# A list scheduler that counts TensorE's instructions in blocks of 256

## The chip, the cores and the metric

The kernel runs on one core of one Trainium2 chip. The metric is the time of one execution on the device in microseconds (us), as the median of several runs. Beside it stands one execution that the hardware profiler took, whose span runs from the first to the last instruction of the program.

## The reference

Four layers run one after the other on a sequence of 2048 rows with 512 columns, each as x = x + layer(layernorm(x)). Layer A multiplies a two-dimensional spectrum by a learned filter; layer B is a long convolution, whose kernel K is made from a state-space model and is the same in both B layers.

```python
def _A_ref(x, w_r, w_i):
    X = rfft2(x) * (w_r + 1j * w_i)
    return irfft2(X, s=(S, D))

def _B_ref(u, A_re, A_im, B_re, B_im, C_re, C_im, log_dt, Dskip):
    dt = exp(log_dt)[:, None]
    P = exp((dt * A)[:, :, None] * arange(L))
    K = einsum("dn,dnl,dn->dl", C, P, dt * B).real
    Kf, Uf = rfft of K and of u, both padded to 2L
    return irfft(Uf * Kf)[:L] + u * Dskip

x = x + _A_ref(_layernorm(x), ...)
x = x + _B_ref(_layernorm(x), ...)
x = x + _A_ref(_layernorm(x), ...)
x = x + _B_ref(_layernorm(x), ...)
```

Here A, B and C in the einsum are complex. All inputs and the output are float32.

## The kernel before

Every Fourier transform is written as matmuls with small tables of cosines and sines, in two factors with a product by twiddles between. The whole of x stays on chip; spectra and intermediate tiles go through DRAM and come back in another layout.

The work is cut into pieces, each a Python generator that yields what its next step needs: an engine's name, a buffer ring, a bank of PSUM, or an event. The class Clock keeps a rough time for each engine (`free`), for each buffer and for the transfers (`land`, with eight transfers open at once). `run` looks for the pieces whose next step could start soonest, takes the one of lowest rank among those within 0.1 us of the earliest, emits its instructions, and lets `note` move the engines' times on. Nothing of this runs on the chip: it only settles in which order each engine's instructions stand, and the chip then follows that order engine by engine, waiting on semaphores. So a number in Clock changes the program only by the order that comes of it.

One thing depends on these times beside the order. Where `run` sees that TensorE would stand idle for over a microsecond before its next step, `fill` puts in matmuls of a 128x128 table on itself (L398), whose result nobody reads. There are 245 of them in the program.

The pieces that the prediction speaks of belong to layer B, which runs twice (r = 0 and r = 1, with r = 1 near the end of the program). The 512 columns go in two halves, e = 0 and e = 1.

- `forward_b`, eight steps b per half: matmuls of the normed x (L813), two copies by ScalarE (L815), and a transfer to DRAM (L831), issued by ScalarE for odd b, otherwise by SyncE (SP).
- `group_b`, eight groups q per half: the spectrum, 16 matmuls (L846); two products with the convolution's spectrum by VectorE (L945); their sum and difference by GpSimd (L951); 32 matmuls back (L962), into all four PSUM banks of their kind; four copies by ScalarE (L971).
- In the layer r = 0 with e = 1 each group also makes its part of the convolution's spectrum: SP loads it from the tile yk into one of three buffers (L924), TensorE runs 16 further matmuls of L846 (on wk), and ScalarE copies the result and stores it (L931, L932). In the layer r = 1 it is loaded (L921).
- `turn_k` makes the last quarter of yk (L1284, stores L1307): none of the loads at L924 may start before all eight stores of it have landed.
- `inv_b`, eight steps b per half: once all eight groups of a half are copied, a load of 512 KB (L981) into one of four buffers, by ScalarE for odd b and by SP otherwise; 8 matmuls (L993); VectorE adds to x (L999); in the layer r = 1 ScalarE issues the store of the result (L1016).

On SP and on ScalarE a transfer that waits for its buffer holds up all that stands behind it. A float32 matmul is carried out in two passes, each with its own load of weights: the trace shows 64 passes for 32 matmuls.

Of the kernel before, what the change touches and what calls it, by code (L numbers as in the profile page):

```python
# [8 lines left out]
BF = mybir.dt.bfloat16  # L9
# [31 lines left out]

RANK = -4, 0.3, 6, 1.2, 25, 0.5, 24, 0.5

NEAR = 0.1

FILL = 1.0, 0.6, 0.25
# [151 lines left out]
class Clock:  # L198
# [4 lines left out]
    def __init__(self, net, last=None):  # L203
        self.net, self.n = net, len(net.nc.cur_bb.bb.instructions)
        self.free, self.seen, self.events, self.marks, self.drops = {}, {}, {}, [], []
        self.held, self.slots, self.land, self.piece, self.table, self.form = {}, {}, 0.0, None, "", None
        self.pools = []
        self.lanes = last.lanes if last else [0.0] * 8
        if last:
            self.free, self.seen, self.events, self.land, self.table = last.free, last.seen, last.events, last.land, last.table  # L210

            self.held = {k: h for k, h in last.held.items() if h[0] in ("ge", "gl", "kh")}
            self.slots.update((k, last.slots[k]) for k in ("ge", "gl", "kh"))
# [68 lines left out]
    def take(self, engine, start, us):  # L282
        self.free[engine] = start + us

    def note(self, ready):

        listed = self.net.nc.cur_bb.bb.instructions
        end = ready
        for ins in listed[self.n:]:
            if not ins.outs or not hasattr(ins.outs[0], "bass_ap"):  # L290
                continue
            engine = {"Activation": "ACT", "Pool": "POOL"}.get(ins.engine.name, ins.engine.name)
            if engine not in COST:
                continue
            aps = [(a.bass_ap, w) for l, w in ((ins.ins, False), (ins.outs, True)) for a in l if hasattr(a, "bass_ap")]
            boxes = [(a.tensor.name, self.boxes(a), w) for a, w in aps]
            start = self.free.get(engine, 0.0)
            for name, box, w in boxes:
                for other, t, v, by in self.seen.get(name, ()):
                    if (w or v) and t > start and (w != v or box[0][2] > 1) and engine != by and self.meet(box, other):  # L300
                        start = t
            out = ins.outs[0].bass_ap
            n = max(int(np.prod([b for _, b in a.ap[1:]])) for a, _ in aps)
            fixed, each, hop = COST[engine]
            if ins.opcode.startswith("DMA"):
                both = all(str(a.space) != str(DRAM) for a, _ in aps)
                start = max(start, self.lanes[0])
                self.land = max(self.land, start) + out.nbytes() / RATE[both]
                done = self.land + LAND
                self.lanes = self.lanes[1:] + [done]  # L310
                self.take(engine, start, COST["SP"][0])
            else:
                if engine == "PE":
                    n = int(np.prod([b for _, b in out.ap[1:]]))
                    stat, rows = aps[1][0], out.ap[0][1]
                    if aps[0][0].dtype == BF:
                        each *= 0.25
                    elif rows < 128:
                        fixed, each = fixed + (0.015 if rows > 32 else -0.005), each * max(rows, 32) * stat.ap[0][1] / 128 ** 2
                    elif stat.ap[0][1] < 128:  # L320
                        fixed, each = fixed + 0.03, each * stat.ap[0][1] / 128
                    elif stat.ap[-1][0] > 2:
                        each *= 2
                    form = rows, stat.ap[0][1]
                    fixed, self.form = fixed + 0.1 * (form != self.form), form
                elif engine == "ACT":
                    each *= 1.75 if out.ap[-1][0] > 8 else 1.55 if len(aps) > 3 else 1
                    f = str(ins.func).split(".")[-1] if ins.opcode == "Activation" else "Copy"
                    if f not in (self.table, "Copy", "Identity", "Abs", "Square"):
                        fixed, self.table = fixed + 1.28, f  # L330
                elif engine == "DVE":
                    wide = sum(int(np.prod([b for _, b in a.ap[1:]])) > 1 for a, _ in aps)
                    memory = not any(str(a.space) == str(PSUM) for a, _ in aps)
                    if ins.opcode == "Reciprocal":
                        each = 6.3
                    elif ins.opcode == "TensorScalarPtr" and wide < 3 and memory:
                        fixed, each = fixed + 0.13 * (len(aps) > wide), 0.53
                    if memory and ins.opcode[:2] != "BN":
                        for a, b in self.pools:
                            start = b if a <= start < b else start  # L340
                if engine == "POOL":
                    self.pools = self.pools[-15:] + [(start, start + fixed + each * n / 1000)]
                self.take(engine, start, fixed + each * n / 1000)
                done = self.free[engine] + hop
            for name, box, w in boxes:
                self.seen.setdefault(name, []).append((box, done, w, w and engine == "PE" and engine))
                if len(self.seen[name]) > 48:
                    self.seen[name] = [e for e in self.seen[name] if e[1] > ready - 3]
            end = max(end, done)
        self.n = len(listed)  # L350
        for key in self.marks:
            self.events.setdefault(key, []).append(end)
        self.marks = []
        return end
# [46 lines left out]
    def run(self, plan):  # L401

        pieces = [[rank, i, 0.0, (), piece] for i, (rank, piece) in enumerate(plan)]
        while pieces:
            ready = [(t, p) for p in pieces if (t := self.time(p[2], p[3])) is not None]
            assert ready, [p[4].__name__ for p in pieces]
            now = min(t for t, _ in ready) + NEAR
            t, p = min((e for e in ready if e[0] <= now), key=lambda e: e[1][:2])
# [1117 lines left out]
```

## Time and profile before

| | us |
|---|---|
| three runs | 768.06, 772.99, 772.9 |
| median of the runs | 772.9 |
| the profiled execution, its own time | 770.48 |
| span of the profiled execution | 768.7 |

The mean clock that TensorE was granted in the span is 0.978 of full speed. In a row of the timeline stand the start, the time that it took, the engine, the line, the operation, the tiles, the shape and the number of passes; in brackets follows the idle time of the engine just before and what ended it. "issue" there is time for which the profile shows nothing that the engine waited for. PE is TensorE, PEld its loads of weights, DVE VectorE, ACT ScalarE, POOL GpSimd. A q after an engine's name is its sequencer, which issues transfers.

### The profile page before, as it was taken

The page shows a single profiled execution, that of the slowest core. Times are in us where ns is not written, and L with a number is a line of the kernel's source. Part 1 is how long each engine was busy: PE and PEld are TensorE (multiplying, and loading weights), DVE is VectorE, ACT ScalarE, POOL GpSimd, SP SyncE. Part 2 cuts the span into 40 slices and gives each one's busy share as a digit, 9 for nine tenths or more (in the row PEclk, how much of TensorE's full clock was granted, in tenths as well). Part 3 has the DMA queues.
Part 4 walks back from the last instruction along what each step waited for, and adds up shares of the span by engine and source line. Part 5 has one row for each costly group of instructions (what it writes and reads, how often), then busy time and mean ns, then how long its engine had stood idle before and what let it go on. Part 6 is the DMA issues. An engine that isn't in the chain of part 4 may idle for free. (4 is left out here: it accounts for less than half of the span.)

```text
span 768.7 us, 24184 instructions
## 1 busy us (share of the span) xinstructions
PE 675.8 (88%) x10382; PEld 460.0 (60%) x10382; DVE 494.8 (64%) x896; ACT 416.1 (54%) x759; POOL 305.0 (40%) x339
## 2 busy tenths in 40 slices
PE   7989998898998899897998789888898999897986
PEld 6877766656565444555455446777777645553666
DVE  6596877957966858863453534876676688275613
ACT  5776998798897797644333032275543434232120
POOL 3921454616625333300343322274544652086310
PEclk9999999999999999999999899999999999999899
DMA  9705312451442977359897953920667235966749
GB/s 331 243 22 177 118 43 104 138 171 69 137 141 95 323 226 237 113 166 239 200 268 226 267 150 89 302 113 4 240 240 245 80 85 122 210 201 182 197 103 285
DMA packets 76699, 132.56 MB, mean 172 GB/s; under 512 B 4684, under 2 KB 53584, under 8 KB 75952
## 3 DMA queue, kind: packets, MB, share of 16 engines
q1 hardware_dynamic: 59184, 103.74, 43.5%
q10 hardware_dynamic: 17408, 27.27, 13.4%
q8 instruction: 82, 1.34, 0.7%
q14 instruction: 25, 0.20, 0.1%
HBM read 70.31 MB, written 27.13 MB: 127 GB/s over the span
## 5 line engine op out<-in xcount | busy, mean ns | idle before, releaser
L1203 POOL TENSOR_TENSOR Y<-wk,Y 128x1024 f32<-128x1024 f32 x32 | 64.5, 2016 | 91.8 <-issue 37.6
L951 POOL TENSOR_TENSOR wk<-wk 128x512 f32<-128x512 f32 x32 | 40.0, 1271 | 113.4 <-DVE wk L945 111.3
L398 PE MATMUL ps<-cRa 128*128 128x128 f32 x490 | 68.7, 288 | 6.4 <-DMA cRa<-in_cRa_dram 4.6
L398 PEld LDWEIGHTS ps<-cRa 128*128 128x128 f32 x490 | 60.8, 196 | 21.0 <-issue 13.9
L945 DVE TENSOR_TENSOR wk<-ps,Y 128x1024 f32<-128x1024 f32 x32 | 37.5, 1218 | 55.5 <-PE ps L846 33.8
L993 PE MATMUL ps<-wk,cRbT 64*128 64x256 f32 x512 | 61.6, 387 | 7.1 <-DMA wk<-Ya 6.2
L815 ACT COPY wk<-ps 128x512 f32<-128x512 f32 x64 | 36.9, 589 | 52.8 <-PE ps L813 43.6
L993 PEld LDWEIGHTS ps<-wk,cRbT 64*128 64x128 f32 x512 | 52.2, 190 | 17.0 <-issue 10.9
L813 PE MATMUL ps<-wk,cRb 128*32 128x256 f32 x1024 | 59.8, 381 | 1.4 <-DVE wk L538 1.0
L1188 DVE SCALAR_TENSOR_TENSOR wk<-wk,ps 128x1024 f32<-128x1024 f32 x32 | 38.8, 1214 | 28.9 <-ACT wk L1186 28.8
L945 DVE TENSOR_TENSOR Y<-ps,wk 128x1024 f32<-128x1024 f32 x32 | 37.4, 1219 | 26.9 <-issue 23.8
L1172 ACT ACTIVATE Y<-ps 128x1024 f32<-128x1024 f32 x48 | 46.6, 1027 | 8.0 <-PE ps L1156 7.9
L813 PEld LDWEIGHTS ps<-wk,cRb 128*32 128x32 f32 x1024 | 34.9, 109 | 26.2 <-DVE wk L538 3.4
L999 DVE TENSOR_TENSOR x<-x,ps 128x256 f32<-128x256 f32 x64 | 24.8, 408 | 38.7 <-PE ps L993 38.5
L762 PE MATMUL ps<-cDaT,apart 128*32 128x256 f32 (+1 forms) x256 | 46.0, 328 | 1.4 <-DVE wk L1227 0.9
L951 POOL TENSOR_TENSOR wk<-Y 128x512 f32<-128x512 f32 x22 | 27.5, 1274 | 45.5 <-DVE Y L945 37.1
L1216 PEld LDWEIGHTS ps<-Y 128*32 128x32 f32 x2048 | 31.2, 112 | 23.7 <-issue 14.0
L1156 PE MATMUL ps<-wk,Y 96*128 96x512 bf16 x128 | 40.2, 388 | 5.5 <-DVE Y L1199 3.8
L971 ACT COPY Ya<-ps 128x256 f32<-128x256 f32 x64 | 19.3, 386 | 44.4 <-PE ps L962 29.3
L1216 PE MATMUL ps<-Y 128*32 128x64 f32 x2048 | 36.3, 223 | 7.7 <-POOL Y L1204 2.8
L1191 ACT ACTIVATE wk<-wk,quarter 128x1024 f32<-128x1024 f32 x32 | 36.8, 1148 | 8.7 <-DVE wk L1189 8.6
L962 PE MATMUL ps<-wk,Y 32*32 32x256 f32 x1344 | 34.8, 399 | 7.6 <-issue 3.9
(218 smaller groups left out, 1668.7 us busy)
## 6 DMA issues: line engine op xcount, KB each, us to landing
Y<-in_GA_dram SPq DMA_DIRECT2D x12, 899.0 KB, 9.3
x<-in_PA_dram SPq DMA_DIRECT2D x16, 642.0 KB, 3.9
x<-in_A_x_dram SPq DMA_DIRECT2D x16, 512.0 KB, 9.5
wk<-yk SPq DMA_DIRECT2D x16, 512.0 KB, 12.5
wk<-khat SPq DMA_DIRECT2D x16, 512.0 KB, 6.5
yk<-wk SPq DMA_DIRECT2D x24, 256.0 KB, 2.9
kd<-wk SPq DMA_DIRECT2D x4, 1024.0 KB, 3.9
khat<-wk SPq DMA_DIRECT2D x8, 512.0 KB, 4.4
```

The source lines that it names most:

```text
L398: self.net.nc.tensor.matmul(p[:, :128], R, R, start=True, stop=True)
L762: nc.tensor.matmul(p[32 * i:32 * i + 32, o:o + n], self.folded(r, i)[:, b, s2].rearrange("p g m -> p (g m)"), self.DaT[:, b, first:first + ...
L813: self.nc.tensor.matmul(p[o:o + 32, 256 * h:256 * h + 256], self.Rb[:, 2 * h + j, 32 * a:32 * a + 32], xn[s], start=True, stop=True)
L815: self.nc.scalar.copy(y[:, j, :], p)
L945: nc.vector.tensor_tensor(t[c], x, kh[:, :, ::-1, :] if c else kh, op=OP.mult)
L951: nc.gpsimd.tensor_tensor(Z[:, :, c], t[0][:, :, c], t[1][:, :, c], op=op)
L993: nc.tensor.matmul(q[s], self.RbT[o, i, :], y[o, i, :], start=i == 0, stop=i == 3)
L1156: self.nc.tensor.matmul(p, f[:, c:c + 128], self.oh[:k, o:o + 512], start=True, stop=True)
L1172: nc.scalar.activation(m[:, :, 1024:] if i == 2 else m[:, i, :1024], p.rearrange("p (i m) -> p i m", i=2) if i == 2 else p, AF.Exp)
L1188: nc.vector.scalar_tensor_tensor(s, c, MAGIC, p, op0=OP.subtract, op1=OP.subtract)
L1203: nc.gpsimd.tensor_tensor(E[:, 0, :1024], c, m[:, :1024], op=OP.mult)
L1216: nc.tensor.matmul(pk[32 * j:32 * j + 32, 64 * e:64 * e + 64], E1[:, r, i, :], E2[:, r, i], start=r == 0, stop=r == 1)
```

## The change

`note` now calls a new method `words` for each step of TensorE. It adds the step's instructions, two for a bfloat16 matmul and four for any other, to a count. When the count passes 256, the step may start no sooner than a time that was noted at the block before; and a new such time is noted for the next block: 2 us behind the later of this start and `land`, the time at which the last transfer that has been issued so far will be in. No instruction, wait or transfer is added or taken away by hand. `last.fetch` carries the count over from the first half of the program to the second.

```diff
+FETCH = 256
 NEAR = 0.1
...
         self.pools = []
+        self.fetch = last.fetch if last else [0, 0.0, 0.0]
...
+    def words(self, start, n):
+
+        self.fetch[0] += n
+        if self.fetch[0] >= FETCH:
+            self.fetch[0] -= FETCH
+            start = max(start, self.fetch[2])
+            self.fetch[1:] = start, max(start, self.land) + 2.0
+        return start
...
+                if engine == "PE":
+                    start = self.words(start, 2 if aps[0][0].dtype == BF else 4)
                 if engine == "POOL":
```

Up to the tail of the convolution's kernel the order stays as it was, and so it does from the second layer A to the start of the last layer B. GpSimd's order is the same throughout. What moves lies in three places: two groups of matmuls near the end of the kernel's making change places, and both layers B are ordered anew. Of the matmuls at L398 199 stand there in place of 245, and 45 of the 46 that are missing belong to the first layer B, the last to the second. In the changed file each line stands 13 lower: L398 is L411, L846 is L859, L962 is L975, L981 is L994, L993 is L1006.

In the first layer B, on TensorE, the piece around the first five inverse steps, before (8 matmuls of L993 are one step):

```order
L846 MATMUL ps<-Ya,Y 32x256 x16
L846 MATMUL ps<-wk 32x256 x16
L993 MATMUL ps<-wk,cRbT 128x256 x8
L846 MATMUL ps<-Ya,Y 32x256 x16
L993 MATMUL ps<-wk,cRbT 128x256 x8
L398 MATMUL ps<-cRa 128x128 x3
L993 MATMUL ps<-wk,cRbT 128x256 x16
L846 MATMUL ps<-wk 32x256 x16
L962 MATMUL ps<-wk,Y 32x256 x32
L846 MATMUL ps<-Ya,Y 32x256 x16
L962 MATMUL ps<-wk,Y 32x256 x32
L993 MATMUL ps<-wk,cRbT 128x256 x8
```

and the same piece now:

```order
L859 MATMUL ps<-wk 32x256 x32
L859 MATMUL ps<-Ya,Y 32x256 x16
L975 MATMUL ps<-wk,Y 32x256 x32
L859 MATMUL ps<-Ya,Y 32x256 x16
L1006 MATMUL ps<-wk,cRbT 128x256 x40
L859 MATMUL ps<-wk 32x256 x32
L975 MATMUL ps<-wk,Y 32x256 x32
L859 MATMUL ps<-Ya,Y 32x256 x16
```

The five inverse steps stand in one row of 40 matmuls, the groups before and behind them are drawn together, and the three matmuls of L398 are gone.

On SP, the loads of yk (L924) and those of the inverse steps (L981) at the same place, before:

```order
L924 DMA wk<-yk 128x2x512
L981 DMA wk<-Y 128x1x1024 x3
L924 DMA wk<-yk 128x2x512 x2
L981 DMA wk<-Y 128x1x1024
L924 DMA wk<-yk 128x2x512 x2
```

and now:

```order
L937 DMA wk<-yk 128x2x512 x2
L994 DMA wk<-Y 128x1x1024 x2
L937 DMA wk<-yk 128x2x512 x2
L994 DMA wk<-Y 128x1x1024 x2
L937 DMA wk<-yk 128x2x512
```

One load of yk moves ahead of the first loads of the inverse steps, one of the inverse loads moves behind two loads of yk, and another load of yk moves ahead of the last pair.

In the second layer B, on TensorE, where the groups of the half e = 1 meet the inverse steps of e = 0, before:

```order
L846 MATMUL ps<-Ya,wk 32x256 x16
L993 MATMUL ps<-wk,cRbT 128x256 x16
L846 MATMUL ps<-Ya,wk 32x256 x16
L993 MATMUL ps<-wk,cRbT 128x256 x16
L846 MATMUL ps<-Ya,wk 32x256 x16
L962 MATMUL ps<-wk,Y 32x256 x32
L846 MATMUL ps<-Ya,wk 32x256 x16
L962 MATMUL ps<-apart,Y 32x256 x32
L993 MATMUL ps<-wk,cRbT 128x256 x8
```

and now:

```order
L975 MATMUL ps<-wk,Y 32x256 x32
L1006 MATMUL ps<-wk,cRbT 128x256 x8
L859 MATMUL ps<-Ya,wk 32x256 x16
L1006 MATMUL ps<-wk,cRbT 128x256 x32
L859 MATMUL ps<-Ya,wk 32x256 x16
L975 MATMUL ps<-wk,Y 32x256 x32
L859 MATMUL ps<-Ya,wk 32x256 x16
L975 MATMUL ps<-apart,Y 32x256 x32
```

The last of the five inverse steps of the half moves up to the other four, ahead of the groups that it followed.

## The prediction

> **What bounds the kernel now.** I read the page first, for how full each engine is and what the instruction queue moves.
>
> ```profile
> PE 675.8 (88%) x10382; PEld 460.0 (60%) x10382; DVE 494.8 (64%) x896; ACT 416.1 (54%) x759; POOL 305.0 (40%) x339
> ...
> q8 instruction: 82, 1.34, 0.7%
> ```
>
> TensorE is busy for 88% of the span. Its matmuls and loads of weights are 2 x 10382 = 20764 instructions, and the queue of instructions moved 82 packets: 253 instructions to a packet, so blocks of 256 with some waits in them fit. Then the windows of the two places that the change orders anew, the first layer B and the end of the second.
>
> ```profile
> 404.00:428.00 24.00, 15.77 (x466) 9.53 (x456) 7.07 (x6) 7.84 (x19) 8.98 (x8) 0.93 0.86 237
> 428.00:455.00 27.00, 24.58 (x469) 14.94 (x464) 14.85 (x26) 5.54 (x12) 7.50 (x6) 0.88 0.82 229
> 455.00:476.00 21.00, 18.19 (x476) 11.43 (x474) 7.07 (x6) 7.69 (x22) 7.49 (x6) 0.99 0.23 74
> 701.00:741.00 40.00, 34.36 (x788) 21.91 (x782) 17.98 (x23) 9.65 (x33) 18.05 (x15) 0.91 0.64 161
> ```
>
> After the length come busy times of TensorE, its loads, VectorE, ScalarE and GpSimd, then the granted clock, the share of the DMA engines and GB/s. Until 455 the transfers fill 0.82 to 0.86 of the DMA engines, then 0.23, while TensorE is never idle for long: up to 455 two things could bound this stage, behind it TensorE's order alone. The timeline of TensorE shows where it stands still.
>
> ```profile
> 418.53 0.88 PE L846 MATMUL ps<-Ya,Y 64*32 64x256 f32 x23 [1.40 <-issue]
> 419.04 0.38 PE L846 MATMUL ps<-wk 64*32 64x256 f32 x1
> 419.18 0.45 PE L846 MATMUL ps<-Ya,Y 64*32 64x256 f32 x7
> 419.26 1.23 PE L846 MATMUL ps<-wk 64*32 64x256 f32 x31
> 420.42 1.50 PE L962 MATMUL ps<-wk,Y 32*32 32x256 f32 x64
> 421.84 0.62 PE L846 MATMUL ps<-Ya,Y 64*32 64x256 f32 x2
> 427.84 1.53 PE L846 MATMUL ps<-Ya,Y 64*32 64x256 f32 x23 [5.38 <-issue]
> ...
> 429.18 2.33 PE L846 MATMUL ps<-wk 64*32 64x256 f32 x31
> ...
> 451.45 1.31 PE L846 MATMUL ps<-wk 64*32 64x256 f32 x24 [2.33 <-issue]
> ```
>
> Both of the first holes lie inside a row of like matmuls, with nothing that they wait for, and between them stand 23+1+7+31+64+2 = 128 passes, with their loads 256 instructions: one block. So these are waits for instructions, 9.1 us in this stage. The queue of SP shows what each stood behind.
>
> ```profile
> 404.05 0.36 SPq L924 DMA_DIRECT2D wk<-yk  x1
> ...
> 416.93 3.35 SPq L981 DMA_DIRECT2D wk<-Y  x3
> 420.39 5.19 SPq L924 DMA_DIRECT2D wk<-yk  x2
> 439.33 0.54 SPq L981 DMA_DIRECT2D wk<-Y  x1
> 439.92 2.65 SPq L924 DMA_DIRECT2D wk<-yk  x2
> ```
>
> The block that begins at 418.53 asks for the next one just when the inverse steps' loads of 512 KB have been issued; it comes 9.3 us later. The hole at 451.45 follows loads at 439.33 and 439.92 likewise. For the second place there is the chain of work that ended last (it begins at 533.93 only).
>
> ```profile
> 704.74 1.74 PE ps L962 x49
> 706.48 3.66 issue
> 710.14 1.09 PE ps L962 x10
> ...
> 725.93 0.99 ACTq L1016
> ...
> 727.48 2.03 PE ps L962 x57
> ...
> 741.77 11.33 DMA wk<-Ya
> ```
>
> Again a hole of 3.66 us, then a wait of 1.63 for ScalarE's copies, which stood behind stores of the result in ScalarE's queue, and at the end the loads of the last half. What ends earlier before 741 ends the kernel earlier.
>
> [...]
>
> **The change part by part.** No instruction is added; all comes from the order.
>
> *The two groups at the end of the kernel's making.* The same steps change places within some 10 us. I take 0, ends -1 and +1.
>
> *The first layer B up to 404.* TensorE has the same work before the last L1284, and the first load of yk waits for the last store of that row (404.05). 45 of the 46 matmuls of L398 that go stand in this layer, with two passes each. Their cost:
>
> ```profile
> 457.68 1.83 PE L398 MATMUL ps<-cRa 128*128 128x128 f32 x14
> ...
> 404.00:428.00 24.00, 3.48 (x24) 2.90 (x24) 0.93 0.86 237
> 428.00:476.00 48.00, 7.40 (x52) 6.25 (x52) 0.93 0.56 162
> ```
>
> The first row is of the timeline, 0.13 us a pass; the others are the windows of L398 alone. Those before 404 cover a wait for transfers and are worth nothing: TensorE will be idle there in their place. A hole of 1.40 (at 418.53) may fall into that wait; I take -1 for this part, ends 0 and -2.
>
> *The hole of 5.38.* Counting four instructions to a matmul along the rows, the start of a block that stood at 427.84 now falls at the end of the spectrum of group 2, and the block before it begins just behind the last group of the first half, whose copies release the loads L981. So the large hole comes again, at about the same time: 0, ends -3 and +4.
>
> *From there to the end of the stage.* It lasts from 427.84 to the first step L993 of the next stage, with these rows in it:
>
> ```profile
> 437.27 3.72 PE L993 MATMUL ps<-wk,cRbT 64*128 64x256 f32 x32
> 440.92 1.09 PE L846 MATMUL ps<-wk 64*32 64x256 f32 x32
> ...
> 452.69 2.38 PE L962 MATMUL ps<-wk,Y 32*32 32x256 f32 x64
> ...
> 456.25 1.50 PE L962 MATMUL ps<-wk,Y 32*32 32x256 f32 x64
> ...
> 460.39 0.73 PE L962 MATMUL ps<-wk,Y 32*32 32x256 f32 x32 [0.89 <-POOL wk L951]
> ...
> 474.34 0.73 PE L962 MATMUL ps<-wk,Y 32*32 32x256 f32 x32 [0.50 <-POOL wk L951]
> 475.00 1.35 PE L993 MATMUL ps<-wk,cRbT 64*128 64x256 f32 x10
> ```
>
> Before: 11 sets of L846 at 1.09, 7 of L962 at 1.50 and 5 inverse steps at 1.86 are 31.8 us. The stage takes 475.00 - 427.84 = 47.2. The other 15.4 are L398 (7.4), the hole of 2.33, six waits for GpSimd and ScalarE (2.8, the first and last shown) and slow passes behind holes (2.9; 2.38 against 1.50). Now one spectrum of L846 more is done ahead of the hole, and part of another, so 9 sets remain: 9.8 + 10.5 + 9.3 = 29.6, with 18 passes of L398 (2.6). The hole, the waits and the slow passes I keep: 2.3 + 2.8 + 2.9. That makes 40.2, a gain of 7.0. Ends: -2, if all of L398 was cover and waits take its place; -15, if hole, waits and slow passes go too.
>
> Behind TensorE here stand ScalarE's copies, and behind these the loads of the next stage, so it moves with this end.
>
> *The second layer B.* The fifth inverse step moves ahead of the groups. The block now begins about as the loads L981 are issued, not after, so its hole of 3.66 should go; but the first inverse step then waits for its own load, which landed some 7.5 us after its issue, of which groups cover about 5. The copies behind ScalarE's stores come later than the stores, so most of the 1.63 goes as well: -3.66 - 1.63 + 2.5, about -3. Ends: +3 (a larger hole in the next block) and -6 (all of it goes and the wait is covered).
>
> The sum: 0 - 1 + 0 - 7 - 3 = -11. From the profiled execution's own 770.5 (span 768.7) that gives 759.5. The median of the runs, 772.9, is 2.4 above the profiled one and the lowest run 2.4 below it, so I forecast 760.
>
> **The rivals.** *Transfers set the end.* All eight loads of yk, eight stores of the spectrum and eight loads of the inverse steps, 12.6 MB, pass between 404 and 455 at 229 to 237 GB/s, 53 us if nothing else moves; the new order moves the same bytes. For it speaks 0.82 to 0.86; against it, that TensorE needs 21 us more behind 455, at 0.23. Then L398's place is taken by waits, the first layer gives 2 and the second nothing: 768 to 769.
>
> *The fifth step's load holds TensorE.* The inverse steps have four buffers, so the fifth load starts when the first step is done, in the first layer on SP behind two loads of yk; and TensorE stands with groups ready behind it. The DMA issues give the times to landing:
>
> ```profile
> wk<-yk SPq DMA_DIRECT2D x16, 512.0 KB, 12.5
> ...
> wk<-Y SPq DMA_DIRECT2D x8, 512.0 KB, 11.9
> ...
> 667.33 3.53 PE L846 MATMUL ps<-Y 64*32 64x256 f32 x64 [2.06 <-DMA Ya<-wk]
> ```
>
> Three steps cover 5.6 us. With 11.9 to landing, and 5.2 more for the issue at 420.39 in the first layer, the waits are 11.5 and 6.3. Each idle time of 2 us or more brings slow passes (3.53 against twice 1.09): 1.4 each. That is 20.6 less the 11 of the forecast: 780. It decides from a landing of about 10 us on, where it takes the whole gain. Against it: by then the first four loads are in, and a load into a quieter queue lands sooner.
>
> [...]
>
> [...] A hole of 5.38 us is followed by 31 passes in 2.33 us against 1.23 before it. [...]
>
> **How the numbers follow.** The forecast has 0.58, the transfers 0.24, the waits that are not there 0.06, the fifth load 0.12. The own range of the forecast is 750 to 766: its lower end with the hole of 2.33, the waits and 2 us of the second layer gone too, its upper with +4 at the large hole and half of the second layer's gain. The range for 8 in 10 is 750 to 776; it holds the two cases without change and stops short of 780. One per cent, about what a measurement of this kernel can tell from no change, is 7.7 us around 772.9: faster is below 765.2. That is the forecast's 0.58; the same are the 0.24 and 0.06, so 0.30; slower 0.12.
>
> **What would show it.** Right: in the new profile the stage from the first load of yk to the first matmul of the following stage is 7 to 9 us shorter, L398 has 398 passes, one hole of 4 to 8 us remains inside a row of L846 or L962 near the loads of the inverse steps, and in the last layer no hole of over 3 us stands between those loads and the next copies. Wrong: TensorE waiting for a load at the row of five inverse steps, or waits of several us for the loads of yk where L398 stood, or holes as many and as long as before.

## The result and the profile after

| | before | after |
|---|---|---|
| median of 20 runs each, us | 771.27 | 763.22 |
| lowest to highest, us | 765.94 to 776.4 | 755.68 to 768.87 |
| span of the profiled execution, us | 768.7 | 763.5 |
| granted clock over the span | 0.978 | 0.974 |

The ratio of the runs is 0.9889, with a 95% interval of 0.9865 to 0.9913: the changed kernel is 6.7 to 10.4 us faster. Ratios here and below compare fast runs alone, without executions at a lower granted clock (one of the 20 of the changed kernel, 768.87 at 0.967), so they can differ from the ratio of the medians. All its lines stand 13 lower (L846 is L859, L962 is L975, L993 is L1006, L398 is L411, L924 is L937, L981 is L994, L1016 is L1029).

The page of the changed kernel, TensorE's busy time and the queue of instructions:

```profile
PE 669.8 (88%) x10290; PEld 452.5 (59%) x10290; DVE 496.0 (65%) x896; ACT 416.7 (55%) x759; POOL 305.1 (40%) x339
...
q8 instruction: 81, 1.33, 0.7%
```

TensorE has 92 passes fewer, all of them L398 (490 before, 398 now). To see where they went, take the first layer B as one window, from its first pass of L846 to the first pass of the long row of inverse steps that ends it; this window is called the stage below. Of before, all instructions and then L398 alone:

```profile
363.83:475.00 111.17, 95.50 (x2141) 55.54 (x2141) 49.11 (x59) 32.73 (x80) 39.95 (x32) 0.94 0.76 204
...
363.83:475.00 111.17, 17.82 (x124) 14.97 (x124) 0.94 0.76 204
```

Of the changed kernel the same window and L411 alone:

```profile
366.21:472.78 106.57, 89.33 (x2050) 49.09 (x2051) 49.51 (x59) 32.76 (x81) 39.94 (x32) 0.89 0.81 215
...
366.21:472.78 106.57, 5.63 (x34) 4.57 (x34) 0.89 0.81 215
```

The first number behind the length is TensorE's busy time. The stage is 4.6 us shorter, and the sum shows three things. L398 went from 17.82 to 5.63: 12.2 less. Idle time, the length less the busy time, went from 15.67 to 17.24: 1.6 more. And the remaining passes, the same 2016 in number, went from 95.50 - 17.82 = 77.7 to 89.33 - 5.63 = 83.7: 6.0 more, at a granted clock of 0.89 in place of 0.94. So idle time was not what the new order took away. These are two profiles; the table behind the experiments has nine.

What TensorE waited for in this window, before and after, by the view of waits (total us, times, longest):

```profile
PE ps L846 <- issue: 13.0, 4, 5.4
PE ps L962 <- POOL wk L951: 2.9, 6, 0.9
```

```profile
PE ps L859 <- issue: 9.7, 3, 5.3
PE ps L975 <- issue: 4.6, 5, 2.1
PE ps L975 <- ACT Y L984: 3.3, 1, 3.3
...
PE ps L975 <- POOL wk L964: 0.7, 2, 0.4
```

"issue" is time in which TensorE waited for nothing that the profile shows; inside a row of like matmuls it is a hole. The sums are 13.0 before and 9.7 + 4.6 after, but 3.86 and 3.47 of them stand just ahead of the first pass of the window; inside it the holes are 9.1 before and 10.8 after. The change plans for these waits, yet as many remain. The timeline of TensorE shows them, and what became of the places that the prediction spoke of:

```profile
393.51 2.35 PE L975 MATMUL ps<-wk,Y 32*32 32x256 f32 x46 [3.33 <-ACT Y L984]
397.94 1.11 PE L975 MATMUL ps<-wk,Y 32*32 32x256 f32 x18 [2.08 <-issue]
...
425.59 1.28 PE L975 MATMUL ps<-wk,Y 32*32 32x256 f32 x39 [0.77 <-issue]
...
429.07 1.07 PE L859 MATMUL ps<-Ya,Y 64*32 64x256 f32 x25 [0.31 <-ACT Y L944]
435.45 1.07 PE L859 MATMUL ps<-Ya,Y 64*32 64x256 f32 x7 [5.31 <-issue]
...
440.54 9.27 PE L1006 MATMUL ps<-wk,cRbT 64*128 64x256 f32 x80
...
456.59 0.71 PE L975 MATMUL ps<-wk,Y 32*32 32x256 f32 x27 [0.73 <-issue]
...
472.78 1.57 PE L1006 MATMUL ps<-wk,cRbT 64*128 64x256 f32 x12
```

The large hole is there again, 5.31 us, inside a row of L859 (25 passes, hole, 7 passes). The five inverse steps at 440.54 run in one row with no wait. From the end of the large hole to the end of the stage it takes 472.78 - 435.45 = 37.3 us, against 47.2 before. The queue of SP says what stood in flight:

```profile
407.58 0.36 SPq L937 DMA_DIRECT2D wk<-yk  x1
...
424.07 1.25 SPq L994 DMA_DIRECT2D wk<-Y  x2
428.00 2.45 SPq L937 DMA_DIRECT2D wk<-yk  x2
442.60 4.31 SPq L994 DMA_DIRECT2D wk<-Y  x2
```

From the first load of yk to the end of the stage it is 472.78 - 407.58 = 65.2 us, before 475.00 - 404.05 = 70.95.

In the second layer B nothing was gained: from its first spectrum to the last row of group matmuls it takes 735.28 - 662.10 = 73.2 us, before 739.71 - 667.33 = 72.4. The timeline of TensorE and that of ScalarE in the changed kernel, where before the hole of 3.66 and the wait of 1.63 stood:

```profile
707.94 0.70 PE L1006 MATMUL ps<-wk,cRbT 64*128 64x256 f32 x3
711.26 6.85 PE L1006 MATMUL ps<-wk,cRbT 64*128 64x256 f32 x61 [2.62 <-issue]
...
723.49 2.91 PE L975 MATMUL ps<-apart,Y 32*32 32x256 f32 x64 [1.91 <-ACT Ya L984]
```

```profile
719.16 3.77 ACTq L1029 DMA_DIRECT2D out_dram<-x  x2
722.97 1.20 ACT L984 COPY Ya<-ps 128x256 f32<-128x256 f32 x4 [17.47 <-DMA wk<-Y]
```

A hole of 2.62 now stands inside the second of the five inverse steps, and the copies at 722.97 still stand behind two stores of the result.

### The profile page after: what moved, and what is told of

It is laid out like the page before. It is cut to its first block, busy times and chain, and to the rows that moved or that the text cites. A ratio compares the mean times of both kernels' runs of the same rounds, so it can differ in the third digit from the quotient of the medians.

```text
span 763.5 us, 24003 instructions
## 1 busy us (share of the span) xinstructions
PE 669.8 (88%) x10290; PEld 452.5 (59%) x10290; DVE 496.0 (65%) x896; ACT 416.7 (55%) x759; POOL 305.1 (40%) x339
## 5 line engine op out<-in xcount | busy, mean ns | idle before, releaser
L964 POOL TENSOR_TENSOR wk<-wk 128x512 f32<-128x512 f32 x32 | 39.9, 1273 | 107.6 <-DVE wk L958 98.4
L1006 PE MATMUL ps<-wk,cRbT 64*128 64x256 f32 x512 | 60.6, 382 | 8.2 <-DMA wk<-Ya 5.0
L1006 PEld LDWEIGHTS ps<-wk,cRbT 64*128 64x128 f32 x512 | 52.3, 187 | 16.6 <-issue 9.1
L411 PE MATMUL ps<-cRa 128*128 128x128 f32 x398 | 57.3, 294 | 4.7 <-DMA cRa<-in_cRa_dram 4.7
L411 PEld LDWEIGHTS ps<-cRa 128*128 128x128 f32 x398 | 51.4, 203 | 15.4 <-issue 9.2
L975 PE MATMUL ps<-wk,Y 32*32 32x256 f32 x1344 | 38.1, 409 | 9.8 <-issue 5.4
L964 POOL TENSOR_TENSOR wk<-Y 128x512 f32<-128x512 f32 x22 | 27.5, 1273 | 45.1 <-DVE Y L958 33.7
L1169 PE MATMUL ps<-wk,Y 96*128 96x512 bf16 x128 | 40.3, 388 | 5.6 <-DVE Y L1212 3.8
L984 ACT COPY Y<-ps 128x256 f32<-128x256 f32 x64 | 19.3, 389 | 41.5 <-PE ps L975 34.9
```

The source lines that it names most:

```text
L411: self.net.nc.tensor.matmul(p[:, :128], R, R, start=True, stop=True)
L964: nc.gpsimd.tensor_tensor(Z[:, :, c], t[0][:, :, c], t[1][:, :, c], op=op)
L975: nc.tensor.matmul(v[j][h][i:i + 32], gi[o:o + 32, j, 4 + 2 * s + c, :], Z[o:o + 32, j, c, :], start=c == 0, stop=c == 1)
L1006: nc.tensor.matmul(q[s], self.RbT[o, i, :], y[o, i, :], start=i == 0, stop=i == 3)
L1169: self.nc.tensor.matmul(p, f[:, c:c + 128], self.oh[:k, o:o + 512], start=True, stop=True)
```

## The experiments

To mix the two orders, the kernels below take the steps from a written list in place of the planner's choice. The list has two parts, one for each call of `run`, and names for each step its piece, its buffers and the matmuls of L398 ahead of it. With the list of before it gives the instructions of the kernel before, with that of after those of the changed kernel.

```diff
     def run(self, plan):
-            now = min(t for t, _ in ready) + NEAR
-            t, p = min((e for e in ready if e[0] <= now), key=lambda e: e[1][:2])
...
+        for step in ORDER[self.turn].split():
+            i, slot, fill = step.split(":")
+            p = pieces[int(i)]
```

At several points both kernels have done the same steps, in another order, so that a stretch of one list can stand in the other. In these kernels L839, L955, L986, L917 and L393 are the L846, L962, L993, L924 and L398 of before (two lines lower in the two kernels that are moved by half a block); likewise L944, L964 and L974 are L951, L971 and L981, and L924 where it names a copy by ScalarE is L931.

**The changed order in the first layer B alone.**

```diff
-ORDER = before[0], before[1]
+ORDER = before[0], before[1][:180] + after[1][180:356] + before[1][356:]
```

> The changed order in the first layer B alone (from the first loads of yk and the turns that go before them to the first step of the following stage, 176 steps of the list, with 17 matmuls of L398 instead of 62); everywhere else the order of before. Theory A (the gain comes from this stage, and what the two traces gave back elsewhere is no gain): 8 us less than before, ratio 0.988 to 0.992, as much as the whole change. Theory B (the prediction's sum: first layer 8, second layer 3): the same here, 8 less, and then some 3 us more in the changed kernel than here. Theory C (the gain is spread over many small moves): 3 to 5 less. In the profile, by A and B: the stage ends 7 to 10 us earlier, a hole of 4 to 6 us remains inside a row near the loads of the inverse steps.

Measured: 0.992 of before (0.9884 to 0.9956), a median of 761.3 us. The window of the stage:

```profile
365.61:469.37 103.76, 89.66 (x2050) 49.84 (x2050) 49.99 (x59) 32.55 (x80) 40.09 (x32) 0.90 0.82 221
```

It is 7.4 us shorter than that of before. So most of the gain comes from this stage, as theories A and B have it. The runs alone don't exclude theory C: of its 3 to 5 us, 3.4 to 5 lie inside the interval (3.4 to 8.9 us). And not all that this profile gains is in the stage: the second layer B, whose order is untouched, takes 69.5 us in it for 72.4 before (a table below has this length for other kernels).

**The changed order at the end of the kernel's making alone.**

```diff
-ORDER = before[0], before[1]
+ORDER = after[0], before[1]
```

> The changed order at the end of the kernel's making alone (two stretches of the list, 25 and 12 steps); everywhere else the order of before, with 444 matmuls of L398. Theory A: 0 to +2 us, since the profile of the changed kernel lost 1.8 us between 257 and 301 with a new idle time of 0.90 us. The prediction's term: 0, ends -1 and +1. Rival: a part of the gain comes from here, -2 to -4, if what TensorE does later in the first layer B is set by the copies and stores that this stage issues.

Measured: 1.0023 (0.9983 to 1.0062), of 771.3 us so 1.3 us less to 4.8 more. No gain comes from here. (The expectation gives a count of 444 for L398; it stands at 490 passes, as before.)

**The changed order in the second layer B alone.**

```diff
-ORDER = before[0], before[1]
+ORDER = before[0], before[1][:867] + after[1][867:]
```

> The changed order in the second layer B alone (the last 144 steps of the list); everywhere else the order of before. The prediction's term: -3 us (ends +3 and -6). Theory A, from the two traces (72.7 us before, 73.5 after in this layer): -1 to +1, the hole of 3.66 us goes and a hole of 2.6 us and a wait of 1.9 us come in its place. Rival: the block boundaries lie elsewhere here than in the changed kernel, since the 46 matmuls of L398 that stand ahead are not gone, so the same order has other holes and gives up to 3 either way.

Measured: 1.005 (1.0011 to 1.0089), slower by 0.8 to 6.9 us. The timeline of TensorE, at the place where the changed kernel has 2.62:

```profile
708.26 0.72 PE L955 MATMUL ps<-wk,Y 32*32 32x256 f32 x27
714.25 2.14 PE L955 MATMUL ps<-wk,Y 32*32 32x256 f32 x37 [5.26 <-issue]
```

The same order has another hole at another matmul, and a longer one: 45 matmuls of L398 that the changed kernel leaves out in the first layer are still ahead of it. This is the rival of the expectation, with a loss.

**The order of before without L398 in the first layer B.** The 62 matmuls of L398 there are left out; nobody reads their result.

```diff
-ORDER = before[0], before[1]
+ORDER = before[0], before[1][:180] + [no_fill(s) for s in before[1][180:356]] + before[1][356:]
```

> The order of before, with the 62 matmuls of L398 in the first layer B left out (they write a bank that nobody reads) and no other step moved. Theory A (the gain comes from the order and the holes; the matmuls of L398 mostly covered waits): -1 to -3 us of the 8. Rival (the matmuls of L398 stood on the path, and the new order gains by having fewer of them): -6 to -8, as much as the change. Third: without them TensorE is idle for longer and runs slower behind the waits, 0 to +3.

Measured: 1.0001 (0.9967 to 1.0036). The window of the stage, and the first two rows of its waits:

```profile
365.38:472.47 107.09, 82.92 (x2016) 43.10 (x2017) 49.40 (x59) 32.83 (x80) 39.95 (x32) 0.90 0.80 216
```

```profile
PE ps L955 <- POOL wk L944: 7.0, 8, 2.6
PE ps L986 <- issue: 4.5, 1, 4.5
```

Without L398 the idle time is 107.09 - 82.92 = 24.2 us, against 15.7, and the waits for GpSimd are 7.0 in place of 2.9; the same 2016 passes take 82.9 in place of 77.7. Of the 17.8 us that L398 took, 13.7 came back as waits and slower passes in this profile, and the runs show no gain over the whole kernel: they exclude the 8 us. In the changed kernel the waits for GpSimd are 0.7 (3.7 in the profile of its order in this stage alone), with 34 passes of L398 left: other work stands in its place. But the stage itself is not as long as before in this profile. Its 107.09 us lies 4.1 under the 111.17 of before, while the second layer B, where nothing was changed, takes 3.1 more (75.5 for 72.4). So the runs say that the absence of L398 doesn't gain the 8 us over the whole kernel; they don't say that the stage gains nothing by it.

**Half a block further, the changed kernel and the kernel before.** The list stays; of the 24 matmuls of L398 at the start 8 become 40 small ones, so that every later instruction stands 128 further on.

```diff
-        for _ in range(n):
+        for _ in range(n if start else n - 8):
             self.net.nc.tensor.matmul(p[:, :128], R, R, start=True, stop=True)
+        for _ in range(0 if start else 8 + 32):
+            self.net.nc.tensor.matmul(p[:32, :64], R[:, :32], R[:, :64], start=True, stop=True)
```

> The changed kernel, every step in its order, with its instructions moved by half a block: of the 24 matmuls of L398 at the start 8 are replaced by 40 small ones (32 x 64), 32 matmuls or 128 instructions more, in a place where TensorE waits for the first input. Theory A (the holes inside rows are waits for the next 256 instructions): they stand 64 passes earlier in the list than in the changed kernel, so the one of 5.31 us is no longer at the same matmul; the time is that of the changed kernel within 4 us, since the gain comes from real work where L398 stood. Theory B (the gain needs the block boundaries where the list put them): 4 to 8 us more than the changed kernel, near 770. Theory C (holes are not bound to blocks): the hole stays at the same matmul.

> The kernel before, every step in its order, moved by half a block in the same way. Theory A: holes 64 passes earlier in the list; the hole of 5.38 us gets smaller or goes, since its block is asked for before the four loads of the inverse steps are issued, and others come; the time within 4 us of before. Theory B: anything from -6 to +6, as the boundaries happen to fall; a gain of 6 or more would say that the change gained by where the boundaries fell. Theory C: the hole stays at the same matmul and the time is that of before within 1 us.

Measured: 0.9962 (0.992 to 1.0004) for the changed order and 1.0065 (1.0029 to 1.0101) for that of before. Both start later; the first pass of `turn_k` in before and in this version of before:

```profile
150.13 1.99 PE L1284 MATMUL ps<-wk,cRk 128*128 128x512 f32 x4 [2.30 <-DVE Y L1199]
```

```profile
152.25 2.01 PE L1279 MATMUL ps<-wk,cRk 128*128 128x512 f32 x2 [2.29 <-DVE Y L1194]
```

So some 2.1 us, 0.003, of each are the price of the small matmuls, by this pair of profiles. What is left is about 3.5 us for the changed order (0.9962 against 0.9889) and 2.9 for that of before, and each of the two is uncertain by about as much. Between the two the order is worth 0.9962 / 1.0065 = 0.990, as much as without the move. The time of the moved changed kernel alone would speak for theory B: it is 5.6 us above the changed kernel, where theory A gave at most 4 and B 4 to 8. Less the small matmuls it is 3.5, and the kernel before lost about as much by the same move. So theory B falls by the comparison of the two: the gain doesn't need the block boundaries where the list put them.

The large hole of the moved changed kernel, in its timeline:

```profile
430.10 1.43 PE L957 MATMUL ps<-wk,Y 32*32 32x256 f32 x57
435.74 1.07 PE L957 MATMUL ps<-wk,Y 32*32 32x256 f32 x7 [4.21 <-issue]
```

In the changed kernel it stood behind 25 of 32 passes of the row just ahead of this one. It has moved by the 7 that were left and 57 more: 64 passes, half a block (64 earlier and 64 later are the same boundary, of this block or the next). In the kernel before the hole of 5.38 stood behind 2 of the 32 passes of a spectrum of L846; moved, the large hole is this one:

```profile
435.70 3.64 PE L988 MATMUL ps<-wk,cRbT 64*128 64x256 f32 x15 [4.45 <-issue]
```

It stands behind the first pass of the first inverse step, and 30 passes of that spectrum, 32 of the next and this one make 63. Theory C falls: the holes are bound to the count of instructions.

**The two halves of the first layer B.** The list up to the last turns, then from the loads of yk on. The first takes 28 matmuls of L398 away, the second 17; the counts given in the two expectations are not right.

```diff
-ORDER = before[0], before[1]
+ORDER = before[0], before[1][:180] + after[1][180:272] + before[1][272:]
```

> Of the changed order only the first 92 steps of the first layer B (up to the last turns and the last groups before the loads of yk); from there on the order of before. L398 has 462 matmuls. Theory A, from the two traces (the first load of yk was issued 3.5 us later in the changed kernel, and the gain came behind the large hole): 0 to +3 us. The prediction's term for this part: -1, ends 0 and -2. Rival: the early part removes 28 matmuls of L398 that stood on the path, -4 to -6.

```diff
-ORDER = before[0], before[1]
+ORDER = before[0], before[1][:272] + after[1][272:356] + before[1][356:]
```

> The other part alone: up to the last turns the order of before, from the loads of yk to the end of the stage the changed order (84 steps); L398 has 473 matmuls. Theory A: -7 to -10 us, all of the gain. The prediction's term for this part: -7, ends -2 and -15. Rival: the two parts only work together, -2 to -5 here and as much in the other.

Measured: the first half 0.9974 (0.9937 to 1.0011), the second 0.9919 (0.9881 to 0.9957), that is 6.2 us less, 3.3 to 9.2. Most of the gain comes from behind the first loads of yk; the first half gives between 4.9 and nothing. In its profile the stage is as long as with the order of before, 113.1 us, and what is shorter is the second layer B, 68.5, whose order is untouched.

**The changed kernel once more.**

> The changed kernel once more, as a measure for the two others and for what differs from one execution to the next. All theories: 0.989 of before, within 0.004; the stage from the first pass of L839 in the first layer B to the long row of L986 takes 104 to 107 us, as in the two profiles with this order, against 111 to 114 in the four profiles with the order of before.

Measured: 0.9888 (0.9849 to 0.9927); the stage took 470.06 - 364.99 = 105.1 us. The hole, in its timeline:

```profile
433.09 1.07 PE L839 MATMUL ps<-Ya,Y 64*32 64x256 f32 x7 [5.59 <-issue]
```

**Two of the inverse steps' loads later.** The steps that issue the third and the fourth load move back in the list: one behind the next loads of yk on SP, the other behind the next store of khat on ScalarE. TensorE's list is untouched. Once in the changed kernel, once in the kernel with the first layer B alone.

```diff
-ORDER = after[0], after[1]
+x = list(after[1])
+third, fourth = x.pop(load(2)), x.pop(load(3))
+x.insert(after_load_of_yk(6), third)
+x.insert(after_store_of_khat(2), fourth)
+ORDER = after[0], x
```

> The changed kernel, with two of the four loads that the inverse steps of the first layer B issue at once (512 KB each) issued later: the third behind the two next loads of yk, the fourth behind the next store of khat; TensorE's list is the same. Theory A (the block that follows is fetched behind the transfers in flight): the hole of 5.31 us shrinks to 1 to 3 us, since its packet stands behind two of these loads and not four; the third and fourth step wait for their loads for 0 to 2 us; -1 to -4 us against the changed kernel. Rival B (the hole is as long whatever is in flight): no change of the hole, time +0 to +2. Rival C (the loads of yk or the steps become late instead): the hole shrinks and a wait of 2 us or more at the third or fourth step takes its place, -1 to +1.

> The same two loads issued later, in the kernel with the changed order in the first layer B alone (0.992 of before). Theory A: the hole that was 3.56 us there shrinks to 1 to 2 us, 0.988 to 0.990 of before. Rivals B and C: 0.992 to 0.994.

Measured: 0.9869 (0.9826 to 0.9912) and 0.9862 (0.9826 to 0.9898). SP's queue and TensorE's timeline of the first:

```profile
424.81 0.56 SPq L974 DMA_DIRECT2D wk<-Y  x1
428.74 1.48 SPq L917 DMA_DIRECT2D wk<-yk  x2
430.27 11.98 SPq L974 DMA_DIRECT2D wk<-Y  x2
```

```profile
434.00 1.08 PE L839 MATMUL ps<-Ya,Y 64*32 64x256 f32 x7 [3.12 <-issue]
```

At the same matmul the hole is 3.12 in place of 5.31 and 5.59. That looks like theory A, but two other profiles with this order in the stage, with all four loads issued at once, have it as short, that of the first layer B alone and that of both layers B (below):

```profile
432.77 1.07 PE L839 MATMUL ps<-Ya,Y 64*32 64x256 f32 x7 [3.56 <-issue]
```

```profile
428.30 0.64 PE L839 MATMUL ps<-Ya,Y 64*32 64x256 f32 x7 [3.15 <-issue]
```

So 3.12 against 3.15 to 5.59 doesn't show that two loads fewer in flight make the hole shorter. In the second kernel the hole at this matmul is gone, where it was 3.56; that speaks for A, in one profile. Rival C shows beside it, a wait of an inverse step for its load:

```profile
434.70 4.29 PE L986 MATMUL ps<-wk,cRbT 64*128 64x256 f32 x32
443.74 0.80 PE L986 MATMUL ps<-wk,cRbT 64*128 64x256 f32 x2 [4.75 <-DMA wk<-Y]
```

Both kernels have the lowest ratios of all, but 0.9869 and 0.9862 can't be told from 0.9888 and 0.992 by their intervals.

A better sign that the hole hangs on the loads lies in the profiles with the order of before in this stage. In that of the kernel with the end of the making changed, TensorE's timeline and SP's queue at the place of the 5.38 are these:

```profile
426.50 1.14 PE L839 MATMUL ps<-Ya,Y 64*32 64x256 f32 x32
...
431.09 1.09 PE L839 MATMUL ps<-Ya,Y 64*32 64x256 f32 x32
```

```profile
426.89 3.55 SPq L974 DMA_DIRECT2D wk<-Y  x3
```

The row at 431.09 is the one with the 5.38 in before, and it has no wait. The block ahead of it begins 128 passes earlier, at about 426.50, 0.4 us before the loads of the inverse steps are issued; in before it began at 418.53, 1.6 us behind their issue at 416.93. The kernel with the second layer's order alone has the same picture (422.14 and 422.52), and no wait at this place either. These are three profiles of one order in the stage; that the loads' issue makes the difference is argued from their times, since no run moved the loads alone here.

**Both layers B, without the end of the kernel's making.**

```diff
-ORDER = before[0], before[1]
+ORDER = before[0], after[1]
```

> The changed order in both layers B, and the order of before at the end of the kernel's making: the changed kernel without that first part. It asks why the three parts alone (0.992, 1.002 and 1.005 of before) do not make up the 0.989 of the whole. Theory A (the second layer's order is worth nothing, and costs 0.005 only where the 46 matmuls of L398 ahead of it are not gone and the block boundaries lie elsewhere): 0.988 to 0.992. Rival (the second layer's order costs 0.005 anywhere, and the end of the kernel's making gives it back): 0.996 to 0.999.

Measured: 0.9892 (0.9858 to 0.9926), the same as the whole change. The 0.005 that the second layer's order cost alone isn't there once the first layer's order stands ahead of it, and the end of the kernel's making gives nothing back. Theory A. In this profile the fifth inverse step waits for its load:

```profile
442.14 3.53 PE L986 MATMUL ps<-wk,cRbT 64*128 64x256 f32 x16 [1.94 <-DMA wk<-Y]
```

The length of the first layer B, from the first pass of L846 to the long row of inverse steps, in the profiles with each order all through the stage (x_first, x_second and x_tail are the kernels with the changed order in the first layer B, in the second and at the end of the making alone, x_nofill is the one without L398, z_front has the first half alone, y_before128 and y_after128 are moved by half a block, r_after is the changed kernel once more, w_late and w_first_late have the two later loads, u_layers has both layers B):

| order in the stage | lengths in us | mean |
|---|---|---|
| before (before, x_tail, x_second, y_before128) | 111.2, 112.6, 114.2, 111.4 | 112.4 |
| changed (after, x_first, y_after128, r_after, u_layers) | 106.6, 103.8, 103.7, 105.1, 103.8 | 104.6 |

The two groups don't overlap and lie 7.8 us apart. The profile of before happened to be the shortest of its group and that of after the longest of its own, so the 4.6 of their comparison is too small. Over the nine profiles the three terms of the sum are, on the mean: L398 12.2 less (17.7 to 18.7 before, 5.3 to 6.3 changed), idle time the same (15.3 to 17.4, and 14.1 to 17.2), and the 2016 other passes 4.3 more (76.5 to 81.1, and 81.3 to 83.7). The kernel without L398 there, with 107.1, lies between the groups. By this length, so by one profile, the absence of L398 would be worth 5.3 of the 7.8, and the work in its place the other 2.5.

The second layer B, from its first spectrum to the last row of group matmuls, takes this long:

| order in the second layer | matmuls of L398 fewer ahead of it | us |
|---|---|---|
| before (before, x_tail) | 0 | 72.4, 74.0 |
| before (z_front) | 28 | 68.5 |
| before (x_first, w_first_late) | 45 | 69.5, 70.3 |
| before (x_nofill) | 62 | 75.5 |
| changed (x_second) | 0 | 76.2 |
| changed (after, r_after, u_layers, w_late) | 45 | 73.2, 70.0, 72.1, 74.0 |

With one and the same order the layer takes 68.5 to 75.5 us, so differences of a few us here come without any step of the layer being moved. With 45 matmuls fewer ahead, the changed order is not the shorter one.

## Why the prediction was right, and where it was not

The time, 763.2 for a forecast of 760, and the side were as forecast, and the stage was the one named; one term of the sum failed. That the total came so near is in part luck, since its parts differ from one profile of the same order to the next by as much (the second layer B by 70.0 to 74.0 us).

*The end of the kernel's making, 0.* Measured 1.0023, between -1.3 and +4.8 us. It stands, and the whole change does without it.

*The first layer B up to the first load of yk, -1.* The first half alone gave 0.9974, between -4.9 and +0.8. In the two profiles the stage needs 404.05 - 363.83 = 40.2 us up to that load before and 407.58 - 366.21 = 41.4 after. Over the nine profiles the means are 40.8 and 40.3. So nothing is seen to be gained up to there, and -1 can't be told from 0. As the prediction said, L398 was cover here: at 393.51 a wait of 3.33 for ScalarE's copies stands in its place.

*The large hole, 0.* It came again near the loads of the inverse steps, as predicted, with 5.31 and 5.59 for 5.38, and with 3.56 and 3.15 in two more profiles of this order. But the 5.38 was itself not fixed: two of the profiles with the order of before have no hole at that matmul.

*From there to the end of the stage, -7.* The profile gives 37.3 for 47.2, so -9.9, and the second half alone 6.2 less in the runs. What the prediction kept, a hole of 2.33 and waits of 2.8, came out smaller: behind the large hole three holes make 1.7, none over 0.73, and one wait of 0.33 is left. The 18 passes of L398 forecast are there, with 2.5 us for 2.6. The account by L398 was right in size, but the runs qualify the reason. Taking L398 away alone gains nothing over the whole kernel (1.0001), though its stage was shorter in the profile; the changed order, which puts groups and spectra that were ready in its place, gains 8. How the gain divides between the two isn't shown.

*The second layer B, -3.* This is the step that failed. The prediction said that the hole of 3.66 should go because the block begins as the loads are issued, and that most of the 1.63 behind ScalarE's stores goes as well. In the profile a hole of 2.62 (2.90 to 3.55 in three more with both layers changed) stands inside the second inverse step, and the wait is 1.91, behind the stores at 719.16 (0.30 to 1.96 in the three). The rows from the boundary before it show what the prediction had wrong:

```profile
701.70 1.30 PE L859 MATMUL ps<-Ya,wk 64*32 64x256 f32 x32
...
707.94 0.70 PE L1006 MATMUL ps<-wk,cRbT 64*128 64x256 f32 x3
```

Counting 128 passes back from the hole gives a boundary inside the row at 701.70, and 128 more one at about 698.4, as the loads of the inverse steps are issued (698.80). So the block begins where the prediction put it, and the boundary that ends it, at 701.70, is passed without a hole. But the next block then begins behind the loads, and the hole stands at its end: the hole didn't go, it came one block later. The prediction had named this only as its bad end. The order alone cost 0.005. With the rest of the change it can't be told from nothing: 0.9892 with it and 0.992 without, 2.2 us with an interval that holds 0 and the -3, while in the profiles the layer is no shorter with it (70.0 to 74.0, without 69.5 and 70.3).

*The sum.* -11 was forecast, -8 came. The stage's -8 is the 7.8 of the table, so the -3 of the second layer is the difference, as far as the intervals can tell. The start was 1.6 too high as well: 772.9 was the median of three runs, that of twenty is 771.27. The lower end of 750 needs the slow passes (2.9) gone too; the reasons named for it lead to 753.

*The rivals.* That the transfers set the end fell, with a time of 763.2 for its 768 to 769; the windows of the changed kernel show them at 0.92 for 27 us, and TensorE's work behind that:

```profile
404.00:428.00 24.00, 20.41 (x652) 11.27 (x644) 14.04 (x12) 9.23 (x26) 13.50 (x11) 1.00 0.74 226
428.00:455.00 27.00, 21.05 (x420) 13.84 (x408) 12.95 (x25) 6.29 (x12) 6.45 (x6) 0.87 0.92 243
455.00:474.00 19.00, 17.26 (x506) 10.18 (x496) 8.77 (x8) 8.29 (x23) 10.03 (x8) 1.00 0.32 109
```

The prediction had called TensorE never idle for long in its first window of before; with 15.77 us busy of 24.00 that was too strong, but the rival falls by the windows behind it. That the fifth step's load holds TensorE fell by the row of 80 passes at 440.54 without a wait. How near it lay shows the wait of 1.94 for that load in the profile of both layers B, and that of 4.75 for an earlier one in the kernel with the two later loads. By the prediction's own terms this rival takes the 11 us from a landing of 7.1 us on, not of about 10. The slow passes that it adds behind each idle time of 2 us or more did not always follow: behind the 2.13 us ahead of 747.60 in before, 32 passes of L993 took 3.72 us, as the 32 at 437.27 did without a wait. What stood against it is seen in the changed kernel, where the inverse steps' load issued at 424.67 landed after 12.6 us and a later one, issued at 448.11, after 5.9. That the waits are not there, for which 0.06 was set, fell by the moved kernels: a hole that shifts by 64 passes when 128 instructions are put in at the other end of the program is a wait for instructions. The packets of the instruction queue q8 show it too. Counted in steps of 128 passes from the hole, before has 18 blocks that begin between 354.70 and 473.46, and behind the begin of each starts one packet, 0.0 to 7.2 us later; the longest of these times ends in the hole of 5.38, with the packet at 425.7 for a block begun at 418.53. In the changed kernel the only packet between 425.59 and 435.45 starts at 432.6, inside the hole of 5.31. In these two holes, of 5.38 and 5.31 us, the profiles put the share of the DMA engines at 1.04 and 1.02.

*The signs that were named.* L398 has 398 passes, one hole of 4 to 8 us remains, and in the last layer none over 3 is in the profile (3.17 in the second profile of the same kernel). The stretch from the first load of yk to the end of the stage was to be 7 to 9 us shorter; it is 65.2 for 70.95, 5.8 shorter; over the nine profiles the means are 64.3 and 71.6, 7.2 shorter.

What stays open: the planner moves the work because it believes TensorE to be waiting for blocks, and the waits for blocks in this stage stay as they were (9.1, then 10.8). Whether any other delay put at such places would have brought as good an order wasn't tried. Nor is it known how much of the stage's gain is the absence of L398 and how much the work in its place, since the kernel without L398 has a shorter stage and no shorter time.

## What to carry to other kernels

Covering matmuls that nobody reads look like waste on the critical path, but taking them away gave back three quarters of their time as waits and slower passes (13.7 of 17.8 us), and nothing was left of it over the whole kernel. What did gain was an order that also put real work in their place. Where TensorE stands still inside a row of like matmuls, count the passes between two such holes (128 here), and put some instructions in far ahead: if the holes move by that count (64 passes here, for 128 instructions), they are waits for instructions, and an edit ahead of them, even a removal, can move them again (in the second layer's changed order the hole is 5.26 us with the 45 matmuls of L398 ahead, and 2.62 at another matmul in the changed kernel, without them). So a change of order is measured in the kernel in which it is to stand: alone it may show a loss, or a gain, that comes only from where the blocks then fall. And where one order gives holes of 3.15 to 5.59 us at one matmul, a single pair of profiles can't size a hole.

## What the runs showed of the hardware that was not expected

- The large wait for instructions stood where the block before it began 1.6 us behind the issue of the loads of 512 KB (5.38 us), and was absent where that block began 0.4 us ahead of it, in two profiles with the same order. Its size with four loads issued at once varies: 5.31, 5.59, 3.56 and 3.15 us at one matmul. With two of them issued some 5 us later it was 3.12 in one kernel and absent in another.
- Moving all instructions by half a block, with no step in another order, made both orders slower, by some 3 us beyond the 2.1 us of the matmuls put in; the intervals allow nearly nothing and twice as much.
- The granted clock tends to be lower where L398 goes: 0.93 to 0.98 in the four profiles with 124 passes of it in the stage, 0.89 to 0.93 in the five with 34, 0.90 in the one with none. The same 2016 other passes take 76.5 to 81.1, 81.3 to 83.7, and 82.9 us.
